# Four more output buffers, two fewer for loaded k and v, and stores that leave later, in a retention and MLP kernel

## Chip, cores and metric

The kernel runs on one core of one Trainium2 chip. The metric is the device time of one execution in microseconds (us); the runs are summarised by their median. The profile is that of one execution.

## What is computed

Retention with one decay per head, for q, k and v of shape (4, 8, 768, 64), and behind it an MLP with the activation h * tanh(softplus(h)), on 3072 tokens of width 512 and a hidden width of 2048. All inputs and outputs are float32.

```python
for t in range(S):
    state = gamma[None, :, None, None] * state + np.einsum('bhd,bhe->bhde', k[:, :, t], v[:, :, t])
    y[:, :, t] = scale * np.einsum('bhd,bhde->bhe', q[:, :, t], state)
...
h = x @ w_in
sp = np.where(h > 20.0, h, np.log1p(np.exp(np.minimum(h, 20.0))))
g = h * np.tanh(sp)
return (g @ w_out).astype(np.float32)
```

## The kernel before

**Tiling.** The 4 x 768 positions are 24 chunks of 128 (`NCK`), numbered 0 to 23. They are worked through in eleven blocks: block 0 has chunks 0 to 3, and block b from 1 to 10 has chunks 2b+2 and 2b+3. For a block the kernel makes scores and masked products of retention, which give `xt`, the transposed input of the MLP; then the first product (into `h_ps`), the activation on ScalarE (ACT) into `g`, and the second product (into `o_ps`). Both products are done in seven products of blocks instead of eight, after Winograd, which costs sums on VectorE (DVE): `gsum` for the activations, `xt` and `wsum` for the inputs and weights. The results of a block are put into output tiles `osb` of 128 x 512 float32 (256 KB), one for each chunk, and stored.

**The way of a chunk.** q, k and v of a chunk (256 KB each, in the small pieces of 64 or 128 floats that the layout gives) are loaded into the tiles `qf`, `kf` and `vf`. GpSimd (POOL) casts and scales q and v (L440, L459) and k too (L454), or ACT does k (L452). The cast q and k are then transposed by a DMA (`turn_by_dma`, L464) into `qkt`, and v is used as it is. Scores (L507) read `qkt`; outer products for the state (L515) read cast k and v. The scores of a block are made during the block before it or the one before that: those of block 5 (chunks 12 and 13) near 87 us, those of block 6 (14 and 15) near 101, those of block 7 (16 and 17) near 115 and those of block 8 (18 and 19) near 129.

**What sets the order.** The order of instructions on each engine is the order in which the program's text issues them; nothing is rescheduled. All loads, transposes and stores but three small ones go through SP's queue, in that order, and what waits there holds up all that stands behind it. A tile has a fixed number of buffers (`bufs`), used in turn: the writer of a tile waits until the readers of the tile that had the same buffer are done.

**Buffers.** `room` (L154) and `room_pair` (L292) make the load tiles: four buffers for `qf`, six for `kf` and `vf`, one for each chunk. Output tiles come from the pool `op` with five buffers (L69), made in `first_out` (block 0, four tiles, L805), `seven` (blocks 1 to 3, two each, L1078) and `full_out` (blocks 4 to 10, two each, L1194). Counted through, block 0 has tiles 0 to 3, and block b has tiles 2b+2 and 2b+3.

**Stores.** A finished tile is entered into the list `stores`. `store(n)` (L1494) takes the n oldest and issues them; `store_due` (L241) takes all that are due. Before the change block 0's four tiles go in `turn_load` (L1540), which block 1's second product calls; block 1's two in `full_in` of block 3 (L1028); block 2's two in `second_of` (L1535); later blocks' two in `next_one` (L1516), in `full_out` of the block that follows. Block 10 stores its own in parts.

**Loads.** q of chunk 10 is loaded in block 1 by `begin_load` (L186), its k and v by `end_load` (L190), in `turn_load`, behind the transposes of chunks 8 and 9. The rest of the loads go in order of chunks.

Of the kernel before, what the change touches and what calls it, by code (L numbers as in the profile page):

```python
# [10 lines left out]
FP32 = mybir.dt.float32  # L11
# [5 lines left out]
def kernel(  # L17
# [11 lines left out]
    d_model, d_ff = moe_w_in.shape  # L29
    P = 128  # L30
    C = 128
    NCH = S // C
    NCK = B * NCH
    HP = H // 2
    TB = 512
    CPB = TB // C
    BLOCKS = [4] + [2] * ((NCK - 4) // 2)
    first = [sum(BLOCKS[:i]) for i in range(len(BLOCKS))]
# [30 lines left out]
    op = ctx.enter_context(tc.tile_pool(name="rn_o", bufs=5))  # L69
# [53 lines left out]
    ONE, BACK = 3, 4  # L123
# [30 lines left out]
    def room(g):  # L154
        loaded[g] = [
            lpool.tile([P, H // 2, 2, D] if nm == "q" else [P, H, D], FP32, name=nm + "f",
                       tag=nm + "f", bufs=4 if nm == "q" else 6) for nm in "qkv"]

    def pair_src(x, n, a):
        b, c = divmod(n, NCH // 2)  # L160
# [3 lines left out]
    def load_one(g, n, queue):  # L164
        b, c = divmod(g, NCH)
        small = g in (first[8] + 1, first[9] + 1)
        if n == 0:
            src, parts = pair_src(q, *divmod(g, 2)), 2 if small else 1
        else:
            src = (k, v)[n - 1][b, :, c * C:(c + 1) * C].rearrange("h p d -> p h d")  # L170
            parts = 1 if g < first[6] else 4 if small and n == 1 else 2
        size = src.shape[1] // parts
        for h in range(0, src.shape[1], size):
            queue.dma_start(loaded[g][n][:, h:h + size], src[:, h:h + size])

    def load(g):
        room(g)
        for n in range(3):
            load_one(g, n, nc.sync)

    def load_to(g):
        while nload[0] < min(g, NCK):
            load(nload[0])
            nload[0] += 1
# [5 lines left out]
    def end_load(g):  # L190
        for n in (1, 2):
            load_one(g, n, nc.sync)
        nload[0] = g + 1
# [47 lines left out]
    def store_due(now):  # L241
        while stores and stores[0][0] <= now:
            _, dst, osb = stores.pop(0)
            nc.sync.dma_start(dst, osb)
# [47 lines left out]
    def room_pair(n, names="kv"):  # L292
        pairs[n] = {
            nm: [lpool.tile([P, H // 2, 2, D], FP32, name=nm + "f", tag=nm + "f",
                            bufs=4 if nm == "q" else 6) for _ in range(2)]
            for nm in names}

    def load_pair(n, nm, a, queue):
# [428 lines left out]
    def sum_input(n):  # L727
        for _ in range(n):
            input_sums.pop(0)()
# [60 lines left out]
    def kept_sum(src, plus=None):  # L790
        m = op.tile([P, *src.shape[1:]], FP32, name="hsum", tag="hsum", bufs=4)
        if plus is None:
            nc.scalar.copy(m, src)
        else:
            nc.vector.tensor_tensor(m, src, plus, op=ALU.add)
        return m

    def first_out(load_more, cast_qk, cast_v, turn_two, sums, weight):

        hf = d_model // 2  # L800
        banks = {(0, 0): pxps.tile([P, 2, hf], FP32, name="o_ps", tag="px")}
        for ij in ((0, 1), (1, 0), (1, 1)):
            banks[ij] = mmps.tile([P, 2, hf], FP32, name="o_ps", tag="mm")
        open_banks = set(banks)
        osb = [op.tile([P, d_model], FP32, name="osb", tag="osb") for _ in range(CPB)]  # L805

        def mm(ij, x, w, fs=range(FPS)):
            for f in fs:
                for t in range(2):
                    nc.tensor.matmul(  # L810
                        banks[ij][:, t], x(f)[:, t * P:(t + 1) * P], w(f), start=ij in open_banks,
                        stop=f == fs[-1], skip_group_check=True)
                    open_banks.discard(ij)

        def a(i, j):
            return lambda f: gts[0, 2 * j * FPS + f][:, i * 2 * P:(i + 1) * 2 * P]

        def b(i, j):
            return lambda f: wouts[2 * i][:, f, j * hf:(j + 1) * hf]

        def s(i):
            return lambda f: sums[i - 1][:, f]

        def t(i):
            return lambda f: tmats[(i - 1) // 2][:, (i - 1) % 2, f]

        def plain(i, j, n, fs=range(FPS)):
            mm((i, j), lambda f: gts[0, n * FPS + f][:, i * 2 * P:(i + 1) * 2 * P],
               lambda f: wouts[n][:, f, j * hf:(j + 1) * hf], fs)

        def done(i, j, plus=None):
            for n in range(2):
                dst, src = osb[2 * i + n][:, j * hf:(j + 1) * hf], banks[i, j][:, n]
                if plus is None:
                    nc.scalar.copy(dst, src)
                else:
                    nc.vector.tensor_tensor(dst, src, plus[:, n], op=ALU.add)

        mm((0, 0), a(0, 0), b(0, 0))
        m1 = kept_sum(banks[0, 0])  # L840
        mm((0, 1), s(1), t(1))
        m5 = kept_sum(banks[0, 1])
        load_more()
        cast_qk()
        plain(0, 0, 1)
        plain(0, 1, 1)
        weight(0, 2)
        for fs in (range(2), range(2, FPS)):
            mm((0, 0), a(0, 1), b(1, 0), fs)
            mm((0, 1), s(4), b(1, 1), fs)  # L850
        mm((1, 0), s(2), t(2))
        u2 = kept_sum(banks[1, 0], m1)
        weight(0, 1)
        cast_v()
        sum_input(1)
        mm((1, 1), s(3), t(3))
        turn_two()
        cast_wout(3, True)
        open_banks.update(((1, 0), (1, 1)))
        u3 = kept_sum(banks[1, 1], u2)  # L860
        mm((1, 0), a(1, 1), t(4))
        u35 = op.tile([P, 2, hf], FP32, name="hsum", tag="hsum", bufs=4)
        nc.gpsimd.tensor_tensor(u35, u3, m5, op=ALU.add)
        pair_scores(2, 0)
        pair_scores(2, 1)
        sum_input(1)
        turn_both(CPB + 2)
        plain(1, 0, 1)
        plain(1, 1, 1)
        plain(0, 1, 3, range(2))  # L870
        outer_two()
        in_makes[3] = in_sums(3)
        input_sums.extend(in_makes[j][i] for i, j in (
            (0, 3), (1, 3), (2, 3), (3, 0), (3, 1), (3, 2), (3, 3)))
        sum_input(2)
        present_two()
        plain(0, 0, 3, range(2))
        plain(1, 0, 3, range(2))
        y_two()
        plain(0, 1, 3, range(2, FPS))  # L880
        done(0, 1, u2)
        plain(0, 0, 3, range(2, FPS))
        done(0, 0)
        weight(1, 0)
        plain(1, 0, 3, range(2, FPS))
        done(1, 0, u3)
        plain(1, 1, 3)
        done(1, 1, u35)
        for n in range(CPB):
            stores.append((0, out_rows(0, n), osb[n]))  # L890
# [69 lines left out]
    def full_in(blk, last):  # L960
# [64 lines left out]
            fn(p)  # L1025
        if late_k:
            g = first[blk] + 5
            store(2)  # L1028
            cast_k(*late_k.pop(0))
            turn_by_dma(g)  # L1030
            casts_v(g - 1)
            casts_v(g)
            load_to(g + 3)
        settled = last or both
        if both:
            leave(blk)
        if not settled:
            u = held[blk + 1][1]
            g = first[blk + 1]
# [34 lines left out]
    def seven(blk, masks, hooks):  # L1074
# [1 line left out]
        px = pxps.tile([P, hf], FP32, name="o_ps", tag="px")  # L1076
        pb = mmps.tile([P, hf], FP32, name="o_ps", tag="mm")
        osb = [  # L1078
            op.tile([P, d_model], FP32, name="osb", tag="osb") for _ in range(2)]

        def a(i, j):
            return lambda f: gts[blk, j * n + f][:, i * P:(i + 1) * P]
# [57 lines left out]
        if blk < ONE:  # L1140
# [21 lines left out]
            if blk == 1:  # L1162
                g = first[blk] + 4
# [3 lines left out]
            elif late_k:  # L1167
                g = first[blk] + 7
# [23 lines left out]
    def full_out(blk, last):  # L1192
        n, hf = NFB // 2, d_model // 2
        osb = [  # L1194
            op.tile([P, d_model], FP32, name="osb", tag="osb") for _ in range(2)]

        def a(i, j):
            return lambda f: gts[blk, j * n + f][:, i * P:(i + 1) * P]
# [111 lines left out]
    def load_more():  # L1310
        load_last_wout(0)
        load_last_wout(1)
        nload[0] = CPB + 4
        ncast[0] = CPB + 2
        both = range(CPB + 2, CPB + 4)
        for g in both:
            room(g)
        for g in both:
            load_one(g, 0, nc.sync)
            load_one(g, 1, nc.sync)  # L1320
        for g in both:
            load_one(g, 2, nc.sync)
# [137 lines left out]
    def outer_two():  # L1460
        u = u_banks()[1][:1]
        for a in range(2):
            pair_outer(2, u, a)
        pair_state(2, u, 0)
# [29 lines left out]
    def store(n):  # L1494
        for _ in range(n):
            _, dst, osb = stores.pop(0)
            nc.sync.dma_start(dst, osb)
# [8 lines left out]
    def next_one(g):  # L1506
        if g < first[ONE] + 8:
            load_to(g + 3)
        if g < NCK:
            turn_by_dma(g)  # L1510
        if g == first[DEFER] + 6:
            for n in range(2):
                load_one(g + n, 2, nc.sync)
            nload[0] = g + 2
        if g >= first[ONE] + 8:
            store_due(NFB)  # L1516

    def load_qk(g):
        room(g)
# [18 lines left out]
        load(g + 4 + ahead)  # L1538

    def turn_load(g):  # L1540
        store(4)
        turn_by_dma(g)
        turn_by_dma(g + 1)
        end_load(g + 2)
        load_to(g + 4)

    def cast_load(g):
# [119 lines left out]
```

## Time and profile before

| | us |
|---|---|
| median of three runs | 191.6 |
| the three runs | 190.57, 192.59, 191.6 |
| the profiled execution | 190.53 |
| its span, first to last instruction | 188.8 |
| TensorE (PE) busy | 182.9 |
| DVE, ACT, POOL busy | 149.8, 113.2, 66.6 |
| HBM read and written | 27.31 MB, 6.29 MB |

The granted clock of TensorE is full speed in all of it. In the rows of the timeline that follow, the first figure is the start in us from the span's start, the second how long the row lasts, then come the engine (SPq is SP's queue, and a row there lasts as long as the issue does), the line of the code, the operation, output and inputs, how many instructions the row merges, and in brackets idle time of the engine before it with what ended it. DMA landings have their own view: the median time from issue to the last byte.

### The profile page before, as it was taken

To read this page: it belongs to the slowest core of one execution; us is meant where nothing else is said; L and a number is where in the kernel's file an instruction comes from. 1 tells how busy PE (TensorE), PEld (TensorE's weight loads), DVE (VectorE), ACT (ScalarE), POOL (GpSimd) and SP (SyncE) were. 2 spreads that over 40 slices of the span, in tenths; PEclk is the share of its full clock that TensorE was granted. 3 is DMA by queue.
4 is the path that set the end of the run, shared out by engine and by line. 5 is a ranking of instruction groups with operands and counts; after the bars stand their busy time and mean duration, and the time that the engine had idled before them with its cause. 6 is when DMAs were issued, how large, how long until landed. Compare 5 with 4: busy or idle time off the path is not lost.

```text
span 188.8 us, 7962 instructions
## 1 busy us (share of the span) xinstructions
PE 182.9 (97%) x3438; PEld 162.3 (86%) x3438; DVE 149.8 (79%) x318; ACT 113.2 (60%) x217; POOL 66.6 (35%) x95
## 2 busy tenths in 40 slices
PE   7898999999999999999999999999999999999993
PEld 7656478888998998998998998998998998988983
DVE  0888599999987997997898697677698688666862
ACT  3575767263645584884683683673673773874651
POOL 5072000579507525642354714804624800000000
PEclk9999999999999999999999999999999999999999
DMA  5999999999999899999999995995899980301103
GB/s 169 306 314 387 385 386 367 297 316 229 189 240 304 162 218 241 172 227 200 216 191 257 223 216 139 191 229 99 209 188 238 215 155 5 115 3 46 69 3 113
DMA packets 83236, 38.84 MB, mean 206 GB/s; under 512 B 58241, under 2 KB 76289, under 8 KB 83201
## 3 DMA queue, kind: packets, MB, share of 16 engines
q1 hardware_dynamic: 82912, 38.22, 87.7%
q8 instruction: 27, 0.44, 1.0%
q10 hardware_dynamic: 288, 0.11, 0.3%
q14 instruction: 9, 0.07, 0.1%
HBM read 27.31 MB, written 6.29 MB: 178 GB/s over the span
## 4 chain that ended last, share of the span: by engine, by line
PE 90%; DVE 3%; DMA 3%; ACT 1%; issue 1%; SPq 0%; DVEq 0%
PE h_ps L972 30%; PE o_ps L1213 23%; PE h_ps L753 8%; PE o_ps L1096 8%; PE o_ps L810 7%; PE y_ps L621 3%; DMA kf<-in_k_dram 3%; PE h_ps L700 2%; PE at L507 1%; PE u_ps L515 1%; PE t_ps L267 1%; PE at L350 1%; PE y_ps L399 1%; PE h_ps L736 1%; DVE gsum L924 1%
## 5 line engine op out<-in xcount | busy, mean ns | idle before, releaser
L972 PE MATMUL h_ps<-xt,wsum 128*128 128x128 f16 x576 | 37.5, 219 | 0.0
L984 ACT ACTIVATE g<-h_ps 128x512 f16<-128x512 f32 x54 | 30.8, 597 | 7.1 <-PE h_ps L972 7.1
L972 PEld LDWEIGHTS <-wsum 128*128 128x128 f16 x576 | 33.6, 98 | 0.1
L972 PE MATMUL h_ps<-xt,win 128*128 128x128 f16 x432 | 31.2, 219 | 0.0
L972 PEld LDWEIGHTS <-win 128*128 128x128 f16 x432 | 26.4, 98 | 0.4
L1213 PEld LDWEIGHTS <-gsum 128*128 128x128 f16 x232 | 21.5, 98 | 2.7
L1213 PE MATMUL o_ps<-tmat,gsum 128*128 128x256 f16 (+1 forms) x176 | 21.6, 268 | 0.0
L459 POOL TENSOR_TENSOR v<-vf,qvs 128x512 f16<-128x512 f32 x18 | 19.1, 1077 | 3.8 <-DMA vf<-in_v_dram 2.8
L1044 DVE TENSOR_TENSOR h_ps<-h_ps,hsum 128x512 f32<-128x512 f32 x18 | 12.5, 693 | 9.5 <-PE h_ps L972 9.4
L440 POOL TENSOR_TENSOR qk<-qf,qvs 128x512 f16<-128x512 f32 x18 | 19.1, 1062 | 2.4 <-DMA kf<-in_k_dram 1.0
L1015 ACT COPY h_ps<-h_ps 128x512 f32<-128x512 f32 x18 | 10.5, 582 | 13.2 <-issue 8.7
L1213 PEld LDWEIGHTS <-g 128*128 128x128 f16 x184 | 16.5, 98 | 1.6
L679 ACT CAST xt<-y_ps 128x512 f16<-128x512 f32 x16 | 10.8, 738 | 9.9 <-PE y_ps L621 9.9
L753 PE MATMUL h_ps<-xt,win 128*128 128x256 f16 (+2 forms) x164 | 16.3, 259 | 0.0
L753 PEld LDWEIGHTS <-win 128*128 128x128 f16 x164 | 13.5, 98 | 2.7
L1223 ACT COPY snap<-o_ps 128x256 f32<-128x256 f32 (+1 forms) x22 | 8.2, 373 | 11.0 <-PE o_ps L1213 11.0
L1213 PE MATMUL o_ps<-wout,g 128*128 128x256 f16 (+1 forms) x120 | 14.5, 265 | 0.0
L762 ACT ACTIVATE g<-h_ps 128x512 f16<-128x512 f32 x18 | 10.7, 597 | 6.0 <-PE h_ps L753 6.0
L1566 POOL COPY summed<-gsum 128x1 f16<-128x1 f16 x7 | 1.6, 234 | 34.7 <-DVE gsum L933 27.4
L454 POOL TENSOR_TENSOR qk<-kf,qvs 128x512 f16<-128x512 f32 x12 | 12.7, 1054 | 2.1 <-DMA kf<-in_k_dram 1.9
L997 DVE TENSOR_TENSOR hsum<-h_ps,hsum 128x512 f32<-128x512 f32 x18 | 12.4, 686 | 0.9 <-PE h_ps L972 0.2
L810 PEld LDWEIGHTS <-g 128*128 128x128 f16 x120 | 11.4, 98 | 1.7 <-DVE tmat L910 0.2
(130 smaller groups left out, 349.7 us busy)
## 6 DMA issues: line engine op xcount, KB each, us to landing
out_dram<-osb SPq DMA_DIRECT2D x22, 256.0 KB, 3.7
qf<-in_q_dram SPq DMA_DIRECT2D x18, 256.0 KB, 5.2
kf<-in_k_dram SPq DMA_DIRECT2D x14, 256.0 KB, 5.9
vf<-in_v_dram SPq DMA_DIRECT2D x14, 256.0 KB, 5.5
wt<-in_moe_w_out_dram SPq DMA_DIRECT2D x6, 512.0 KB, 8.7
vf<-in_v_dram SPq DMA_DIRECT2D x20, 128.0 KB, 3.9
wi<-in_moe_w_in_dram SPq DMA_DIRECT2D x4, 512.0 KB, 8.7
kf<-in_k_dram SPq DMA_DIRECT2D x16, 128.0 KB, 4.3
```

Source lines behind the costliest of these rows:

```text
L440: nc.gpsimd.tensor_tensor(in_place(q16.rearrange("p (w x) d -> p w x d", x=2)), by_head(qf), scale_by_head(qs_two[:, heads]), op=ALU.mult)
L454: nc.gpsimd.tensor_tensor(dst, src, boosts.rearrange("p (w y) -> p w y", y=2).unsqueeze(3).broadcast_to((P, H // 2, 2, D)), op=ALU.mult)
L459: nc.gpsimd.tensor_tensor(cast[g][2], loaded.pop(g)[2], vs[g % 2].unsqueeze(2).broadcast_to((P, H, D)), op=ALU.mult)
L679: nc.scalar.copy(dst[:, :, x], src)
L753: nc.tensor.matmul(h_ps[:, j, cols], wins[s][f // 2][:, bp, f % 2 * P:(f % 2 + 1) * P], xts[blk][:, bp, cols], start=(bp == 0 and at == 0) ...
L810: nc.tensor.matmul(banks[ij][:, t], x(f)[:, t * P:(t + 1) * P], w(f), start=ij in open_banks, stop=f == fs[-1], skip_group_check=True)
L972: nc.tensor.matmul(o_ps[:, f], w(f // 2, k)[:, f % 2 * P:(f % 2 + 1) * P], x[:, k], start=begin and f == 0 and k == 0, stop=k == 1, skip_g ...
L984: nc.scalar.activation(gt[:, f:f + n, j * C:(j + 1) * C], src, AF.Mish, scale=inv_boost3)
L997: nc.vector.tensor_tensor(m, src, plus, op=ALU.add)
L1044: nc.vector.tensor_tensor(pf[p], pa[p], m5[p], op=ALU.add)
L1096: nc.tensor.matmul(o_ps[:, cols], x(f), w(f)[:, cols], start=first and z == 0, stop=z == n - 1, skip_group_check=True)
L1213: nc.tensor.matmul(o_ps[:, c:c + wide], x(f), w(f)[:, c:c + wide], start=first and f == 0 and c == cols.start, stop=f == n - 1, skip_group ...
```

## The change

`kf` and `vf` get four buffers instead of six; `osb` gets nine instead of five. The four stores are taken out of `turn_load`, and `end_load` of chunk 10 (its k and v) is put ahead of the two transposes there. The pair of stores in `full_in` is split: one goes before the transpose of chunk 13 as before, the other behind the loads of chunks 14 and 15. In `next_one` the stores of blocks 4 to 7 take the two oldest tiles only; from chunk 24 on, all that are left. Since the list of stores is served oldest first, block 0's tiles now go at the places where block 1's and block 2's went, block 1's where block 3's went, and so on, and ten are left for the last call sites.

```diff
@@ room, room_pair
-                       tag=nm + "f", bufs=4 if nm == "q" else 6) for nm in "qkv"]
+                       tag=nm + "f", bufs=4) for nm in "qkv"]
...
@@ first_out, seven, full_out
-        osb = [op.tile([P, d_model], FP32, name="osb", tag="osb") for _ in range(CPB)]
+        osb = [op.tile([P, d_model], FP32, name="osb", tag="osb", bufs=9) for _ in range(CPB)]
...
@@ full_in
         if late_k:
             g = first[blk] + 5
-            store(2)
+            store(1)
             cast_k(*late_k.pop(0))
             turn_by_dma(g)
             casts_v(g - 1)
             casts_v(g)
             load_to(g + 3)
+            store(1)
...
@@ next_one
-        if g >= first[ONE] + 8:
+        if g >= NCK:
             store_due(NFB)
+        elif g >= first[ONE] + 8:
+            store(2)
...
@@ turn_load
     def turn_load(g):
-        store(4)
+        end_load(g + 2)
         turn_by_dma(g)
         turn_by_dma(g + 1)
-        end_load(g + 2)
         load_to(g + 4)
```

SP's queue in block 1's second product, at the transposes of chunks 8 and 9 (the first `qf` is chunk 10's, the one at the end chunk 11's):

```order
 L174 DMA vf<-in_v_dram 128x8x64
 L174 DMA qf<-in_q_dram 128x4x128
-L1497 DMA out_dram<-osb 128x512 x4
+L174 DMA kf<-in_k_dram 128x8x64
+L174 DMA vf<-in_v_dram 128x8x64
 L464 DMA_TRANSPOSE qkt<-qk_1329 128x8x128
 L464 DMA_TRANSPOSE qkt<-qk_1332 128x8x128
-L174 DMA kf<-in_k_dram 128x8x64
-L174 DMA vf<-in_v_dram 128x8x64
 L174 DMA qf<-in_q_dram 128x4x128
 L174 DMA kf<-in_k_dram 128x8x64
```

Four stores are gone from there, and k and v of chunk 10 have moved from behind the transposes to ahead of them.

SP's queue in block 3's first product, from the transpose of chunk 12 to the loads of chunk 16, before the change:

```order
L464 DMA_TRANSPOSE qkt<-qk_1738 128x8x128
L1497 DMA out_dram<-osb 128x512 x2
L464 DMA_TRANSPOSE qkt<-qk_1880 128x8x128
L174 DMA qf<-in_q_dram 128x4x128
L174 DMA kf<-in_k_dram 128x4x64 x2
L174 DMA vf<-in_v_dram 128x4x64 x2
L174 DMA qf<-in_q_dram 128x4x128
L174 DMA kf<-in_k_dram 128x4x64 x2
L174 DMA vf<-in_v_dram 128x4x64 x2
L174 DMA qf<-in_q_dram 128x4x128
```

And after it:

```order
L464 DMA_TRANSPOSE qkt<-qk_1734 128x8x128
L1498 DMA out_dram<-osb 128x512
L464 DMA_TRANSPOSE qkt<-qk_1876 128x8x128
L174 DMA qf<-in_q_dram 128x4x128
L174 DMA kf<-in_k_dram 128x4x64 x2
L174 DMA vf<-in_v_dram 128x4x64 x2
L174 DMA qf<-in_q_dram 128x4x128
L174 DMA kf<-in_k_dram 128x4x64 x2
L174 DMA vf<-in_v_dram 128x4x64 x2
L1498 DMA out_dram<-osb 128x512
L174 DMA qf<-in_q_dram 128x4x128
```

One store stands ahead of chunk 13's transpose instead of two, and one between the loads of chunks 15 and 16; both are of block 0, where before they were of block 1.

More of the change, by code (lines that the diff above doesn't have):

```diff
@@ L294, in room_pair @@
             nm: [lpool.tile([P, H // 2, 2, D], FP32, name=nm + "f", tag=nm + "f",
-                            bufs=4 if nm == "q" else 6) for _ in range(2)]
+                            bufs=4) for _ in range(2)]
             for nm in names}
@@ L1078, in seven @@
         osb = [
-            op.tile([P, d_model], FP32, name="osb", tag="osb") for _ in range(2)]
+            op.tile([P, d_model], FP32, name="osb", tag="osb", bufs=9) for _ in range(2)]
         def a(i, j):
@@ L1194, in full_out @@
         osb = [
-            op.tile([P, d_model], FP32, name="osb", tag="osb") for _ in range(2)]
+            op.tile([P, d_model], FP32, name="osb", tag="osb", bufs=9) for _ in range(2)]
         def a(i, j):
```

## The prediction

> **What bounds the kernel now.** I read the page first: the busy times and the chain that ended last.
>
> ```profile
> span 188.8 us, 7962 instructions
> ...
> PE 182.9 (97%) x3438; PEld 162.3 (86%) x3438; DVE 149.8 (79%) x318; ACT 113.2 (60%) x217; POOL 66.6 (35%) x95
> ...
> PE 90%; DVE 3%; DMA 3%; ACT 1%; issue 1%; SPq 0%; DVEq 0%
> ```
>
> TensorE (PE) is busy for 182.9 of 188.8 us and holds 90% of the chain; the DMA has 3%. The view of busy time by stretches tells where the other 5.9 us lie.
>
> ```profile
> 0.00:8.00 8.00, 6.02 (x67) 5.28 (x68) 2.81 (x6) 3.14 (x5) 2.76 (x17) 1.00 0.80 228
> 8.00:16.00 8.00, 7.18 (x216) 4.51 (x217) 6.84 (x9) 5.79 (x13) 4.14 (x9) 1.00 1.13 326
> ...
> 75.00:90.00 15.00, 14.95 (x357) 13.71 (x355) 13.46 (x27) 10.77 (x22) 6.78 (x9) 1.00 1.21 202
> ...
> 174.00:188.80 14.80, 11.84 (x165) 11.09 (x162) 8.54 (x16) 6.89 (x15) 0.00 (x0) 1.00 0.22 74
> ```
>
> The second figure after the comma-separated length is PE's. It is idle for 1.98 us before 8, 0.82 before 16 and 2.96 after 174: 5.76 of the 5.9, all in stretches that the change doesn't touch. Between 16 and 174 us only 0.1 us is not busy. But a matmul that waits inside a group still shows as busy, so I looked at PE's timeline for groups that start late or last longer than their twins, and found two.
>
> ```profile
> 86.70 0.23 PE L621 MATMUL y_ps<-qkt,mid 64*64 64x64 f16 x8
> 86.98 0.32 PE L621 MATMUL y_ps<-am,v 64*64 64x64 f16 x16
> ...
> 87.38 0.50 PE L507 MATMUL at<-qkt 64*64 64x64 f16 x32
> 87.69 0.34 PE L621 MATMUL y_ps<-am,v 64*64 64x64 f16 x16
> ...
> 128.33 0.23 PE L621 MATMUL y_ps<-qkt,mid 64*64 64x64 f16 x8
> 128.39 0.30 PE L621 MATMUL y_ps<-am,v 64*64 64x64 f16 x16
> ...
> 128.84 0.85 PE L507 MATMUL at<-qkt 64*64 64x64 f16 x32
> 129.52 0.30 PE L621 MATMUL y_ps<-am,v 64*64 64x64 f16 x16
> ```
>
> At 128.33 the masked product (y_ps<-am,v) follows the one before it after 0.06 us; at 86.70 after 0.28 us: a stall of 0.22 us. The 32 score matmuls of L507 give way to the next group after 0.31 us at 87.38 and after 0.68 us at 128.84: a stall of 0.37 us. Sum 0.59 us. These two are all that I find for the change to win on PE after the start.
>
> **What feeds those stalls.** L507 reads transposed q and k, which come through SP's queue; here its rows of before.
>
> ```profile
> 55.44 3.10 SPq L1497 DMA_DIRECT2D out_dram<-osb  x4
> 59.42 3.63 SPq L464 DMA_TRANSPOSE qkt<-qk  x2
> 63.11 0.57 SPq L174 DMA_DIRECT2D kf<-in_k_dram  x1
> 63.74 0.62 SPq L174 DMA_DIRECT2D vf<-in_v_dram  x1
> 64.41 1.14 SPq L174 DMA_DIRECT2D qf<-in_q_dram  x1
> ...
> 72.19 4.87 SPq L464 DMA_TRANSPOSE qkt<-qk  x2
> 77.11 1.32 SPq L174 DMA_DIRECT2D vf<-in_v_dram  x2
> 78.55 2.87 SPq L464 DMA_TRANSPOSE qkt<-qk  x1
> 81.51 1.00 SPq L1497 DMA_DIRECT2D out_dram<-osb  x2
> 82.61 1.36 SPq L464 DMA_TRANSPOSE qkt<-qk  x1
> 84.03 1.04 SPq L174 DMA_DIRECT2D qf<-in_q_dram  x1
> ...
> 119.43 2.00 SPq L244 DMA_DIRECT2D out_dram<-osb  x2
> ...
> 123.49 1.70 SPq L464 DMA_TRANSPOSE qkt<-qk  x1
> ```
>
> The view of DMA issues has, for the transposes at 82.61 and at 123.49:
>
> ```profile
> qkt<-qk SPq DMA_TRANSPOSE x1, 4.6
> ...
> qkt<-qk SPq DMA_TRANSPOSE x1, 5.6
> ```
>
> So the one of chunk 13 lands at 82.61+4.6=87.2, just ahead of the scores at 87.38, and the one of chunk 19 at 123.49+5.6=129.1, inside the scores that began at 128.84: that is the 0.37 us. From 63.11 to 84 the queue's rows follow each other with gaps of under 0.5 us, so there a row waits chiefly for the rows ahead of it.
>
> The other stall hangs on VectorE (DVE), and through it on GpSimd (POOL) and a load.
>
> ```profile
> 81.88 2.04 POOL L459 TENSOR_TENSOR v<-vf,qvs 128x512 f16<-128x512 f32 x2 [2.31 <-DMA vf<-in_v_dram]
> ...
> 83.11 1.09 DVE L924 TENSOR_TENSOR gsum<-g 128x512 f16<-128x512 f16 x1
> 84.59 0.42 DVE L924 TENSOR_TENSOR gsum<-g 128x512 f16<-128x512 f16 x1
> 85.71 1.22 DVE L609 TENSOR_TENSOR am<-at,tri_half 128x1024 f16<-128x1024 f32 x1
> ```
>
> The mask (L609) ends at 86.93 and releases PE at 86.98. Ahead of it one and the same sum took 1.09 us while POOL cast v (81.88 to 83.92) and 0.42 us once POOL was done: 0.67 us too long. POOL began late, having waited 2.31 us for v of chunk 12, issued at 77.11. The Trainium skill, SBUF — State Buffer, section "Who interferes with whom", says that a VectorE operation with two inputs in SBUF and a GpSimd operation that reads SBUF shut each other out through a shared read interface; the two L924 rows agree. By it the 0.22 us go only if the casts end before 83.11 (else the sum below is 190.16, not 189.94), and come back wherever else a cast meets such a sum.
>
> **The change part by part.**
>
> *The four stores of block 0 leave the place at 55.44.* They took 3.10 us of SP's time and 1 MB of traffic. The transposes behind them could not have gone earlier than 59.42 by more than the 0.88 us that SP sat idle after the stores (55.44+3.10=58.54): they wait for the casts of chunks 8 and 9. Gain here nothing: k and v of chunk 10 (0.57+0.62 at 63.11) now fill the gap and lie hidden under that wait.
>
> *k and v of chunk 10 leave the place behind the transposes.* All that follows at 63.11 moves up to 64.41-63.11=1.30 us earlier, since there the queue runs without a pause. If the lighter traffic also shortens the issues, the bound is higher: one store fewer ahead of chunk 13's transpose gives 0.5 us (half of the 1.00 at 81.51), so 1.8 us for that transpose; the upper end is what SP could win until the casts hold it, some 3 us. I take 1.8. The casts of v12 and v13 then run from about 80.6 to 82.6 (81.88-1.30), clear of the sum at 83.11: the 0.22 us go. What is late next is nothing: chunk 13 gains margin instead of losing it.
>
> *The stores lag by four tiles from block 3 on.* In each block two go out as before, but older ones, whose data is long ready. Rows after 106 us hold as many stores at the same places, so the effect there is only what remains of the earlier start; from the row at 119.43, 1 us per pair is issue, not a wait that I can take off. For the transpose at 123.49 to land before 128.84 it has to go 0.3 us sooner. Carry-over of 0 to 1.3 us: I take it to suffice, but casts on POOL come between, and this is the weaker half of the gain. The end gets four stores more around 150 us, at 0.5 us of issue each, with more than 30 us left before the last output: nothing.
>
> *Four buffers instead of six for k and v.* A load of chunk g now waits for the casts of chunk g-4. The tightest that I find, and the output tiles in the same fence:
>
> ```profile
> 78.35 1.23 POOL L459 TENSOR_TENSOR v<-vf,qvs 128x512 f16<-128x512 f32 x1
> ...
> 86.22 1.05 SPq L174 DMA_DIRECT2D vf<-in_v_dram  x2
> ...
> 89.11 0.42 DVE L1111 TENSOR_TENSOR osb<-o_ps,snap 128x256 f32<-128x256 f32 x1 [0.91 <-ACT xt L679]
> ...
> 99.96 0.42 DVE L1236 TENSOR_TENSOR osb<-o_ps,snap 128x256 f32<-128x256 f32 x1
> ```
>
> v of chunk 14 (86.22, at most 3 us sooner: 83.2) needs chunk 10's v, cast by 79.58: 3.6 us of slack. q has had four buffers all along. Cost nothing; if the cover went, every load and transpose behind it in SP's queue would stand too.
>
> *Nine output tiles.* Tile n waits for the store of tile n-9. Block 3's second tile, written at 89.11, needs tile 0, stored where the row at 81.51 stands: 7.6 us. Block 4's first, written at 99.96, needs tile 1, whose store now stands behind chunk 15's loads, at about 91.8: 8.2 us. The stores of before landed as the view of the store line at L244 says:
>
> ```profile
> DMA to landing us min/median/max: 2.0/3.6/5.0
> ```
>
> So 2.6 us of slack at the worst landing seen. Cost nothing.
>
> **The sum.** Profiled execution: 190.53 us, of which 188.8 span and 1.73 around it. 190.53-0.22-0.37=189.94. The runs shown have a median of 191.6, 1.07 above the profiled one, between 190.57 and 192.59. If that excess has nothing to do with the queue, the median after is 191.6-0.59=191.0; if it is the same thin margins missed in other executions, it is 189.94. I take the middle, 190.5.
>
> **Rivals.**
>
> *Nothing arrives* (0.16): from block 4 on the transposes go when POOL's casts release them, so the earlier start is used up before 123.49, and the sum at 83.11 still meets a cast. For it: in the rows after 106 us nothing has moved but older stores. Against: the unbroken queue from 63.11 to 84. Time 191.6.
>
> *The thin margins are the spread* (0.22): chunk 13's transpose lands 0.2 us before its use and chunk 19's 0.3 us after; in slower executions both cost more, and the change cures them and smaller waits of 0.1 to 0.2 us that I can't resolve. Then 189.94 and up to some 0.6 us more: 189.3. PE's 182.9 us speak against more.
>
> *The output tiles block DVE* (0.14, slower): a store that lands later than 7.6 us after its issue, behind transposes and loads, holds DVE at block 3's second tile and at block 4's first; behind them on DVE stand the sums from which PE's next block starts. At two worst landings, 10.0 us, it is 10.0-7.6=2.4 and 10.0-8.2=1.8 us: 191.6+4.2=195.8, or 194.0 for the first alone. For it: the new place of tile 1. Against: 5.0 us is the longest landing seen.
>
> *Earlier casts meet other sums* (0.06): each meeting costs DVE up to 0.67 us, three in the chain of a block 2.0: 193.6, or 192.3 for one block's one.
>
> **How the numbers follow.** The forecast, a gain too small to tell, has 0.42, of which 0.06 lies below 189.7. The measurement tells about 1% from no change, 189.7 to 193.5. Faster: 0.22+0.06=0.28. Slower: 0.14+0.03 (half of the last rival)=0.17. Within: 0.55. The range reaches from 189.2, the second rival, to 192.9, above the first rival and the cheap form of the last; it leaves out the tile rival and a few points below.
>
> **What would show it.** k and v of chunk 10 issue at about 55.4; the queue reaches chunk 13's transpose before 81; POOL casts v12 and v13 before 81; L924 at 83 falls to 0.42; L507 of block 6 gives way after 0.31 us. Wrong if a DVE row that writes osb shows a wait for a store, if a load of k or v waits for POOL, or if PE shows a new idle place before 174 us.

## The result and the profile after

| | before | changed |
|---|---|---|
| median of 13 runs each, us | 191.81 | 190.42 |
| lowest and highest, us | 190.31, 193.28 | 190.04, 190.72 |
| profiled execution, us | 190.53 | 190.19 |
| its span, us | 188.8 | 188.4 |

The ratio is 0.9933, with a 95% interval of 0.9905 to 0.996: the change saves 0.7%, and the runs lie within 0.7 us of each other where those of before lay 3 us apart. Some executions, whatever the kernel, fall into a slower state; they are left out of the times, ranges and ratios that follow. The page of the changed kernel:

```profile
span 188.4 us, 7968 instructions
...
PE 182.7 (97%) x3438; PEld 162.9 (86%) x3438; DVE 148.2 (79%) x318; ACT 113.0 (60%) x217; POOL 66.8 (35%) x95
...
PE 92%; DMA 3%; SPq 1%; POOL 1%; issue 1%; ACT 0%; DVE 0%; POOLq 0%; DVEq 0%
```

Busy times are nearly the same; DVE has 1.6 us less, 0.68 of it in one sum that is shown below. What changed in the chain is that DVE's 3% has gone. In before the chain ran over DVE from 81.85 to 86.94 us, through the sums to block 3's mask; the mask no longer holds PE. PE's timeline of the changed kernel at the two places that the prediction names (start, length):

```profile
86.86 0.23 PE L621 MATMUL y_ps<-qkt,mid 64*64 64x64 f16 x8
86.92 0.30 PE L621 MATMUL y_ps<-am,v 64*64 64x64 f16 x16
...
128.91 0.50 PE L507 MATMUL at<-qkt 64*64 64x64 f16 x32
129.22 0.34 PE L621 MATMUL y_ps<-am,v 64*64 64x64 f16 x16
```

The masked product now follows after 0.06 us (0.28 before), and the scores made in block 6, those of chunks 18 and 19, give way after 0.31 us (0.68 before). Both stalls are gone. SP's queue, same view:

```profile
54.21 2.33 SPq L174 DMA_DIRECT2D qf<-in_q_dram  x1
56.58 0.64 SPq L174 DMA_DIRECT2D kf<-in_k_dram  x1
57.32 0.85 SPq L174 DMA_DIRECT2D vf<-in_v_dram  x1
59.64 2.96 SPq L464 DMA_TRANSPOSE qkt<-qk  x2
62.65 0.58 SPq L174 DMA_DIRECT2D qf<-in_q_dram  x1
...
74.91 1.26 SPq L174 DMA_DIRECT2D vf<-in_v_dram  x2
76.38 2.12 SPq L464 DMA_TRANSPOSE qkt<-qk  x1
78.59 0.52 SPq L1498 DMA_DIRECT2D out_dram<-osb  x1
79.43 1.52 SPq L464 DMA_TRANSPOSE qkt<-qk  x1
...
122.67 1.75 SPq L464 DMA_TRANSPOSE qkt<-qk  x1
```

k and v of chunk 10 fill the gap ahead of the transposes of chunks 8 and 9, which still go at 59.64 (59.42 before). v of chunks 12 and 13 go at 74.91 instead of 77.11, chunk 13's transpose at 79.43 instead of 82.61, and chunk 19's at 122.67 instead of 123.49. On POOL and DVE that gives:

```profile
78.52 3.40 POOL L459 TENSOR_TENSOR v<-vf,qvs 128x512 f16<-128x512 f32 x3
...
83.27 0.41 DVE L924 TENSOR_TENSOR gsum<-g 128x512 f16<-128x512 f16 x1
```

The casts of v end at 81.92, before the sum begins, and the sum takes 0.41 us where it took 1.09.

To see where two executions part, I set the starts of the same groups on PE side by side: here the start of each block's first product (L753 in block 1, L972 from block 2 on), as the shift in us against the changed kernel's profile. A column that grows between two lines has lost that time between them. b1 to b3 and a1 are further executions of the kernel before and of the changed one; they come below.

```
             us, changed  before     b1     b2     b3     a1
17 us (L700)       17.07   -0.28   0.00   0.00  -0.27  -0.28
block 1            47.03   -0.21   0.00   0.22  -0.14   0.02
block 2            61.88   -0.21   0.03   0.25  -0.11   0.05
block 3            76.03   -0.21   0.04   0.44  -0.11   0.04
block 4            90.58    0.01   0.71   1.10  -0.07   0.34
block 5           104.47   -0.06   0.61   1.04  -0.19   0.33
block 6           118.24   -0.06   0.61   1.04  -0.19   0.34
block 7           132.12    0.26   0.61   1.41   0.56   0.33
block 8           145.79    0.26   0.61   1.41   0.55   0.33
block 9           159.47    0.35   0.70   1.50   0.64   0.93
block 10          172.88    0.34   0.70   1.50   0.64   0.93
```

The profiled execution of before lost 0.62 us against the changed one between 17 and 173 us (from -0.28 to 0.34). In the two profiled times it shows as 0.34 only, because the changed kernel's execution had the longer start.

### The profile page after: what moved, and what is told of

Its sections match the earlier page's. It is cut to its first block, busy times and chain, and to the rows that moved or that the text cites. A ratio compares the mean times of both kernels' runs of the same rounds, so it can differ in the third digit from the quotient of the medians.

```text
span 188.4 us, 7968 instructions
## 1 busy us (share of the span) xinstructions
PE 182.7 (97%) x3438; PEld 162.9 (86%) x3438; DVE 148.2 (79%) x318; ACT 113.0 (60%) x217; POOL 66.8 (35%) x95
## 4 chain that ended last, share of the span: by engine, by line
PE 92%; DMA 3%; SPq 1%; POOL 1%; issue 1%; ACT 0%; DVE 0%; POOLq 0%; DVEq 0%
PE h_ps L972 30%; PE o_ps L1214 23%; PE o_ps L1097 10%; PE h_ps L753 8%; PE o_ps L810 7%; PE y_ps L621 3%; DMA kf<-in_k_dram 3%; PE h_ps L700 2%; PE u_ps L515 1%; PE at L507 1%; PE y_ps L399 1%; POOL qk L320 1%; PE h_ps L736 1%; PE t_ps L267 1%; PE at L350 1%
## 5 line engine op out<-in xcount | busy, mean ns | idle before, releaser
L972 PE MATMUL h_ps<-xt,wsum 128*128 128x128 f16 x576 | 37.5, 219 | 0.0
L972 PEld LDWEIGHTS <-wsum 128*128 128x128 f16 x576 | 33.6, 98 | 0.0
L972 PE MATMUL h_ps<-xt,win 128*128 128x128 f16 x432 | 31.2, 219 | 0.0
L972 PEld LDWEIGHTS <-win 128*128 128x128 f16 x432 | 26.4, 98 | 0.4
L753 PE MATMUL h_ps<-xt,win 128*128 128x256 f16 (+2 forms) x164 | 16.3, 260 | 0.0
L753 PEld LDWEIGHTS <-win 128*128 128x128 f16 x164 | 13.4, 98 | 2.7
## 6 DMA issues: line engine op xcount, KB each, us to landing
vf<-in_v_dram SPq DMA_DIRECT2D x20, 128.0 KB, 4.1
kf<-in_k_dram SPq DMA_DIRECT2D x16, 128.0 KB, 4.3
```

Source lines behind the costliest of these rows:

```text
L753: nc.tensor.matmul(h_ps[:, j, cols], wins[s][f // 2][:, bp, f % 2 * P:(f % 2 + 1) * P], xts[blk][:, bp, cols], start=(bp == 0 and at == 0) ...
L972: nc.tensor.matmul(o_ps[:, f], w(f // 2, k)[:, f % 2 * P:(f % 2 + 1) * P], x[:, k], start=begin and f == 0 and k == 0, stop=k == 1, skip_g ...
```

## The experiments

**Where the slower executions of before lose their time: b1, b2, b3.** No edit: the kernel before three times more, for profiles of other executions.

> The kernel before, unchanged, for a profile of another execution. Theory (its runs differ by how late a few transposes land): if this execution takes 191.5 us or more, PE has stalls longer than the 0.22 and 0.37 us of the first profile, in the scores of L507 in blocks 5 to 8 (near 87, 101, 115 or 129 us), which make up the difference. Rival: the difference is spread evenly or lies in the first 47 us.

> The kernel before once more, a second further execution: as for the first, the excess over 190.5 us sits in waits of L507 for transposed q and k between 53 and 145 us (theory), or in the first 47 us or evenly (rival).

> The kernel before once more, a third further execution: as for the first, the excess over 190.5 us sits in waits of L507 for transposed q and k between 53 and 145 us (theory), or in the first 47 us or evenly (rival).

They took 190.9, 191.88 and 191.05 us, so only b2 is over the 191.5 us from which b1's theory was to count. The table has their losses. b3 loses 0.75 us between blocks 6 and 7, b2 0.37 there; b1 and b2 lose 0.67 and 0.66 in block 3. PE's timeline of b3 names the wait:

```profile
128.71 0.27 PE L507 MATMUL at<-qkt 64*64 64x64 f16 x8
129.47 0.51 PE L507 MATMUL at<-qkt 64*64 64x64 f16 x24 [0.49 <-DMA qkt<-qk]
```

After eight of the 32 score matmuls PE waits for chunk 19's transposed q and k. That is the theory's place. But the queue had issued this transpose no later than in the first profile (123.29 against 123.49): it landed later, after 6.1 us against 5.6, in b2 after 5.9. So what stops PE here is a lead that is too short for a landing that varies. The loss in block 3 is not at the theory's place: most of it, 0.5 us, comes in the block's first product, before its scores; the rest is at the masked product, 0.23 in b1 and 0.16 in b2, where the first profile had 0.22. POOL of b1, DVE of b1, and the same DVE line of the changed kernel:

```profile
74.84 1.04 POOL L440 TENSOR_TENSOR qk<-qf,qvs 128x512 f16<-128x512 f32 x1 [1.44 <-PE y_ps L621]
75.84 1.04 POOL L459 TENSOR_TENSOR v<-vf,qvs 128x512 f16<-128x512 f32 x1
```

```profile
76.20 0.83 DVE L958 TENSOR_TENSOR xt<-xt 128x256 f16<-128x256 f16 x1
```

```profile
76.16 0.28 DVE L958 TENSOR_TENSOR xt<-xt 128x256 f16<-128x256 f16 x1
```

POOL stood idle for 1.44 us ahead of the cast of chunk 12's q. The view names PE as the one that ended it; in the first profile of before, POOL's row for the same cast has a load there:

```profile
74.15 1.04 POOL L440 TENSOR_TENSOR qk<-qf,qvs 128x512 f16<-128x512 f32 x1 [1.00 <-DMA kf<-in_k_dram]
```

The data it casts comes through SP's queue. In b1 the load of chunk 12's q, issued at 67.45, landed 7.2 us later, 0.2 us ahead of the cast; in the first profile it went at 67.17 and landed after 6.8, again 0.2 us ahead. So the cast waits for the load, and here too the landing is what came later. So v of chunk 11 was cast from 75.84 to 76.88, on top of the sum at 76.20, which took 0.83 us instead of 0.28; the input sums behind it on DVE feed PE's next products. b2 has the same with 0.90 us. In the changed kernel the two casts of q run back to back from 72.31, and v of chunk 11 is done at 75.37, ahead of the sum. The theory holds in that what comes late comes through the queue; it fell short on how: PE pays by transposes in block 6 and, more often in these three, by casts that meet DVE's sums in block 3. b2 also loses 0.22 us in the first 47 us, where the rival looked, and 0.19 in block 2.

**Buffers alone: e1_buffers.** The old order with nine output tiles and four each for k and v.

```diff
-                       tag=nm + "f", bufs=4 if nm == "q" else 6) for nm in "qkv"]
+                       tag=nm + "f", bufs=4) for nm in "qkv"]
...
-        osb = [op.tile([P, d_model], FP32, name="osb", tag="osb") for _ in range(CPB)]
+        osb = [op.tile([P, d_model], FP32, name="osb", tag="osb", bufs=9) for _ in range(CPB)]
```

> The kernel before with the buffers of the change alone (nine output tiles, four each for k and v) and the old order of the queue. Theory (the gain is the queue's lead over the transposes): nothing moves, ratio 1.000 to the kernel before, a median near 191.8 and runs as far apart as before, over 2 us. Rival (the buffers themselves matter): most of the change's 0.7% is here, a median near 190.4 and runs within 1 us. If four buffers cost something, a load of k or v waits for POOL and the median is above 192.

190.78 us (190.22 to 192.07) against 191.1 for before on that chip; ratio 0.9988, interval 0.9955 to 1.0021. Buffers alone change nothing that can be told, and four for k and v cost nothing that can be told: chunk 13's transpose goes at 82.44, as before. Its profiled execution happened to have no stall, 188.4 us of span, as short as the changed kernel's: in a lucky execution the old order of the queue costs nothing.

**Loads ahead, stores in place: e2_loads.**

```diff
     def turn_load(g):
+        end_load(g + 2)
         store(4)
         turn_by_dma(g)
         turn_by_dma(g + 1)
-        end_load(g + 2)
```

> The kernel before with k and v of chunk 10 loaded ahead of the four stores and the two transposes, the stores staying where they were, and no buffer changed. Theory (the queue's lead): the transposes of chunks 8 and 9 go at 59.4 to 60.0, all behind them about 1 us sooner than before, chunk 13's transpose at about 81.5; about half of the gain, a median of 190.8 to 191.3. Rival (the stores' traffic in the busy stretch is what hurts): no gain, 191.5 to 192.

192.39 us (191.79 to 193.24), ratio 1.0072, interval 1.0045 to 1.0099: slower, which neither theory had. It loses 2.1 us in block 2's first product, 1.7 of it at the start. DVE, then PE:

```profile
63.81 0.42 DVE L1111 TENSOR_TENSOR osb<-o_ps,snap 128x256 f32<-128x256 f32 x1 [2.37 <-DMA out_dram<-osb]
```

```profile
64.49 1.95 PE L972 MATMUL h_ps<-xt,wsum 128*128 128x128 f16 x32 [1.55 <-DVE xt L958]
```

With five output tiles block 1's second tile has the buffer of block 0's first, whose store the loads had pushed back to 58.75; DVE stood 2.37 us for it, and PE behind DVE. This is the prediction's tile rival in the kernel with five tiles: the loads can't go first without more tiles.

**Loads ahead, stores in place, with the buffers: e5_loads_buffers.** The same edit on top of e1_buffers.

> The kernel before with the buffers of the change (nine, four, four) and k and v of chunk 10 ahead of the four stores, which stay ahead of the transposes. Theory (the 2.1 us that the same order lost with five output tiles were the wait of the second tile of block 1 for block 0's first store): that wait is gone, since the tile is a fresh one; but four stores between the loads and the transposes of chunks 8 and 9 hold these back to about 62.7 as they did there, so the rest of the queue gains nothing: 190.8 to 191.8, runs 2 us apart. Rival (the loads' place is the whole of the gain once there are tiles enough): 190.4, runs within 1 us. A transpose of chunk 9 that lands after the scores at 67.65 would show as a wait of L507 there.

191.02 us (190.31 to 192.57), ratio 1.0006, interval 0.998 to 1.0032. The 2.1 us are gone and no gain can be told. Its queue shows why:

```profile
58.41 3.42 SPq L1497 DMA_DIRECT2D out_dram<-osb  x4
61.97 3.36 SPq L464 DMA_TRANSPOSE qkt<-qk  x2
...
82.38 1.52 SPq L464 DMA_TRANSPOSE qkt<-qk  x1
```

The stores hold the transposes of chunks 8 and 9 back from 59.64 to 61.97, so what the loads win at the one end is lost at the other; chunk 13's transpose goes at 82.38, hardly sooner than before. Two rows of this execution show the cost, PE at the scores of chunks 8 and 9 and DVE in block 4:

```profile
67.65 0.63 PE L507 MATMUL at<-qkt 64*64 64x64 f16 x32
```

```profile
96.86 1.03 DVE L924 TENSOR_TENSOR gsum<-g 128x512 f16<-128x512 f16 x1
```

The scores give way 0.57 us after their start, in the changed kernel 0.40: the held-back transpose costs PE 0.17 us, the sign that the expectation names. The sum, 0.42 us in the changed kernel, met a cast of v that ran from 95.57 to 97.62, and PE lost 0.32 us behind it.

**Stores away, loads in place: e3_stores.** The changed kernel with the old place of the loads.

```diff
     def turn_load(g):
-        end_load(g + 2)
         turn_by_dma(g)
         turn_by_dma(g + 1)
+        end_load(g + 2)
```

> The changed kernel with k and v of chunk 10 put back behind the transposes: the stores are gone from there and lag as in the change, the loads don't move. Theory (the queue's lead): the row of chunk 11's q stays near 64.4 and chunk 13's transpose gains only the 0.5 us of the one store fewer and what lighter traffic gives; a quarter to half of the gain, a median of 191.1 to 191.5. Rival (the stores' traffic): all of the gain, 190.4, runs within 1 us.

190.92 us (190.28 to 192.34), ratio 0.9985, interval 0.9958 to 1.0012: no gain that can be told, runs 2 us apart. The rows of its queue, and PE in block 4 and at block 6's start:

```profile
62.77 0.57 SPq L174 DMA_DIRECT2D kf<-in_k_dram  x1
...
82.27 1.43 SPq L464 DMA_TRANSPOSE qkt<-qk  x1
```

```profile
101.91 0.38 PE L507 MATMUL at<-qkt 64*64 64x64 f16 x24 [0.43 <-DMA qkt<-qk]
...
119.23 0.62 PE L972 MATMUL h_ps<-xt,win 128*128 128x128 f16 x8 [0.32 <-issue]
```

The gap that the stores left stays empty, the loads stand behind the transposes, and chunk 13's transpose wins 0.34 us. Here it is chunk 15's transpose that comes late, by 0.43 us. Nearly as much, 0.48 us, goes at block 6's start (119.23), where PE waits for nothing that the profile shows; what cost that half is not known.

**What a late transpose costs: e4_catchup, e4_again.** The changed kernel with all due stores at once at block 4, ahead of chunk 17's transpose; the second is one more execution, whose profile is read here.

```diff
-        if g >= NCK:
+        if g >= first[ONE] + 8:
             store_due(NFB)
-        elif g >= first[ONE] + 8:
-            store(2)
```

> The changed kernel, but at block 4 all tiles that are due are stored at once: six stores near 106 us instead of two, and from there two per block as before. Theory (a transpose that leaves the queue late stops PE by as much): four stores more are 2 us of issue ahead of chunk 17's transpose, which goes at about 113 instead of 111.05 and lands after the scores of block 7 ask for it near 115; PE stalls there by 1 to 2.5 us and the median is 191.3 to 193. Rival (where the stores stand makes no difference): 190.4.

> The changed kernel with six stores at once at block 4, once more, for a profile that can be set beside the others. Theory (a transpose that leaves the queue late stops PE by as much): the transpose of chunk 17 goes at 112.5 to 113.5 and PE waits for it in L507 near 115 us, by 1 to 2 us; from there on all starts shift by as much, and nothing else is late. Rival: the excess over the changed kernel is spread over the blocks, with no wait of L507 over 0.3 us.

191.42 us (190.97 to 193.36), ratio 1.0011 to before (0.9971 to 1.0051): no gain over before can be told; the changed kernel itself did not run on this chip. The profile of e4_again, which took 191.21 us:

```profile
104.72 4.39 SPq L244 DMA_DIRECT2D out_dram<-osb  x6
...
112.29 1.72 SPq L464 DMA_TRANSPOSE qkt<-qk  x1
```

```profile
116.02 0.38 PE L507 MATMUL at<-qkt 64*64 64x64 f16 x24 [0.84 <-DMA qkt<-qk]
```

The transpose goes 1.24 us later than the changed kernel's (111.05), and PE waits 0.84 us for it, and the start of block 6, which had been 0.13 us ahead of the changed kernel's, is 0.85 us behind it. The transpose landed after 3.7 us, at 115.99, and PE went on at 116.02. 0.84 is less than the 1 to 2 us expected, since chunk 17 had some margin. One thing more was late against the expectation: chunk 19's transpose, 5.46 us ahead of its scores, cost PE another 0.2 us.

**The changed kernel again, and without the split: a1, e6_unsplit.** The second has both stores ahead of chunk 13's transpose.

```diff
-            store(1)
+            store(2)
             cast_k(*late_k.pop(0))
...
             load_to(g + 3)
-            store(1)
```

> The changed kernel itself, on the same chip as the next runs, to compare them with. Theory and rival alike: 0.993 of the kernel before, 190.2 to 190.6 us, runs within 1 us of each other, no wait of L507 for a transpose in the profile.

> The changed kernel with both stores of block 3's first product ahead of chunk 13's transpose, as they stood before. Theory (with the lead of 3 us over the scores the half microsecond of one store is within the margin): no difference to the changed kernel, 190.2 to 190.7, chunk 13's transpose at about 79.9 instead of 79.4. Rival (the split is what saves chunk 13): 190.8 or more, with a wait of L507 near 87.5 us.

a1 190.59 us (190.18 to 191.27), ratio 0.9977, interval 0.9955 to 0.9998, where 0.993 was expected; e6_unsplit 190.59 (189.92 to 191.36), 0.9975, 0.9948 to 1.0001. The split makes no difference that can be told: with both stores ahead, chunk 13's transpose goes at 80.56, still 2 us sooner than before. On this chip the kernel before had a median of 190.88, so the gain was 0.2% instead of 0.7%; the changed kernel itself took nearly the same time on both, 190.42 and 190.59. By the traces, what the change is worth depends on how late the old queue's data comes, and that differs from execution to execution; why the old kernel was so much slower on the first chip is not shown. The times also don't tell whether one of the two moves alone has part of the gain: the intervals of e1_buffers, e3_stores and e5_loads_buffers overlap that of a1. For that the rows of the queue are the evidence.

## Why the prediction came out right, step by step

The measured median is 190.42 us against 190.5, in the range, with a gain of 0.7%, under the 1% that it called too small to tell; 13 runs each do tell it. The places and the order of the queue were worked out and came about; that the median fits to 0.1 us is in part luck, as the item on the excess says.

- *PE's two stalls of 0.22 and 0.37 us go*: shown, by the rows at 86.92 and 128.91. The sum of 0.59 us stands against 0.62 us lost between 17 and 173 us.
- *k and v of chunk 10 hide under the wait for the casts, the queue behind moves up*: shown. Neither half does it alone (one profile each, e3_stores and e5_loads_buffers: chunk 13's transpose at 82.27 and 82.38); together they bring 79.43. The term was under-sized: 1.8 us taken, 3.2 measured (82.61-79.43), near the upper end of 3. (k and v themselves issue at 56.58 and 57.32 rather than 55.4.)
- *The 0.22 us hang on the casts of v, which must end before the sum*: shown, though no run moved the cast alone. Where chunk 13's transpose went in its old place, at 82.27 or later, the casts met this sum (L924, near 83 us): in seven profiles, and each time the sum ended 0.28 us after them, whenever it had begun. PE then stalled at the masked product for 0.23 us where the sum lasted 1.11 (b1), 0.22 at 1.09 (the first profile), 0.16 at 1.03 (b2), 0.04 at 0.91 (e3_stores), and at most 0.01 at 0.75 (b3), 0.71 (e1_buffers) and 0.46 (e5_loads_buffers). In the changed kernel's two profiles no cast is there and the sum takes 0.41. The rows agree with the Trainium skill, SBUF — State Buffer, section "Who interferes with whom", in b1 and b2 too, where the sum of xt went from 0.28 to 0.83 and 0.90 us under a cast. L924 in b1, b2, e3_stores, b3 and e1_buffers, in this order:

```profile
83.80 1.11 DVE L924 TENSOR_TENSOR gsum<-g 128x512 f16<-128x512 f16 x1
...
84.26 1.03 DVE L924 TENSOR_TENSOR gsum<-g 128x512 f16<-128x512 f16 x1
...
83.23 0.91 DVE L924 TENSOR_TENSOR gsum<-g 128x512 f16<-128x512 f16 x1
...
83.20 0.75 DVE L924 TENSOR_TENSOR gsum<-g 128x512 f16<-128x512 f16 x1
...
83.31 0.71 DVE L924 TENSOR_TENSOR gsum<-g 128x512 f16<-128x512 f16 x1
```

- *Carry-over to chunk 19, 0 to 1.3 us*: 0.82 us. From issue to the scores the transpose had 5.35 us in before, 5.42 in b3, 5.46 in e4_again and 5.61 in b2: all four stalled. With 5.95 (e3_stores) to 7.0 (a1) none of the others did, among them b1 (6.0) and the changed kernel (6.24). The landing took between 3.6 and 6.1 us, so a lead like the changed kernel's covers the longest one seen. In its first profile the landing was also shorter than in before's, 4.5 against 5.6 us, which the prediction did not have; either alone would have been enough there, by the sum: 122.67+5.6=128.3 or 123.49+4.5=128.0, against scores that begin at 128.91.
- *Four buffers for k and v cost nothing*: no cost can be told in e1_buffers. But one of the prediction's signs of being wrong is there: the view of SP's waits (us in total, times, longest) has a load that waits for POOL, chunk 10's v at 57.32. It is hidden, since the transposes behind it wait for their casts until 59.64; the slack of 3.6 us was worked out for chunk 14 and missed this load, which the change had moved forward.

```profile
SPq L174 <- POOL summed L1568: 0.6, 1, 0.6
```

- *Nine tiles cost nothing*: no DVE row that writes osb waits for a store in the changed kernel. That they are needed was not in the prediction, and e2_loads shows it.
- *The excess of other executions, middle taken between two cases*: nothing in the rows chose the middle, so that it fits is luck. The two cases were 191.0 and 189.94, and the median of before itself moved from 191.6 to 191.81 with ten more runs, and was 190.88 on another chip. The changed kernel's runs lie within 0.7 us on the first chip and 1.1 on the other, those of before within 3.0 and 1.7, so much of the spread went with the change. "These two are all that I find" was true of the one profiled execution only: others lose 0.5 us in block 3's first product.
- *The rivals.* That nothing arrives is refuted by the interval. Thin margins as the cause of the spread was right in kind, too large in size. The tiles blocking DVE, and earlier casts meeting other sums at a price, did not come about in the changed kernel's two profiles; e2_loads and e5_loads_buffers show that both can happen, for 2.1 and 0.32 us.

## What to carry to other kernels

Where an engine is 97% busy, look for groups that last longer than their twins, and profile several executions: a queue that is only just in time costs nothing in the lucky one. In a queue that runs in order, what waits there for nobody (finished stores) belongs behind what others wait for, and a load fits into the idle place ahead of an instruction that has to wait anyway; in the profiles of the two moves taken alone the delay was only passed on. Give a transfer a lead that covers its longest landing, not its usual one. Before a store is put off, count who needs its buffer next.

## What was not expected of the hardware

The start of the kernel comes in two forms that differ by 0.28 us at 17 us, whatever the kernel: before, b3, a1, e6_unsplit and e4_again had the shorter one, the changed kernel's first profile, b1, b2, e1_buffers, e2_loads, e3_stores, e4_catchup and e5_loads_buffers the longer. Part of the lead, 0.07 to 0.33 us, is gone again by block 2.

A transpose's landing is as late as its last part. Each lands with sixteen reports in the trace, and in 210 of the 234 transposes of the thirteen profiles the last comes within 0.1 us of the one before it; in ten it comes 1.5 to 1.65 us later. Four of the ten are chunk 19's, in b1, b2, b3 and e4_again; in b2, b3 and e4_again the other fifteen were there 4.0 to 4.6 us after the issue, ahead of the scores, and PE stalled for the last one. What delays it is open.

And a1, where no transpose was late, lost 0.9 us in two places; PE's timeline:

```profile
87.85 0.38 PE L507 MATMUL at<-qkt 64*64 64x64 f16 x24 [0.19 <-issue]
...
148.94 0.62 PE L972 MATMUL h_ps<-xt,win 128*128 128x128 f16 x8 [0.42 <-issue]
```

In both PE waited for nothing that the profile shows. Chunk 13's transpose had gone at 79.47 and landed 5.4 us later, nearly 3 us before PE stopped at 87.66. What holds PE there, and at 119.23 in e3_stores, stays open, and with it what is left of the spread of the changed kernel.
